# Weight transfers moved away from two rounds of row scatters, and GpSimd's clears and constants moved behind its load requests, in a chunked-attention and top-1 mixture-of-experts kernel

## The chip, the cores and the metric

The kernel runs on one core of a Trainium2 chip. The metric is device time in microseconds of one execution. The time before is 236.27 us, the median of 3 runs (233.84 to 236.61).

The core has five engines with instruction queues of their own: TensorE (PE; its weight loads are shown as PEld), VectorE (DVE), ScalarE (ACT), GpSimd (POOL) and SyncE (SP, which here only issues transfers). Transfers are issued by two of them: SP, whose transfers the profile shows as queue q1, and GpSimd, whose transfers are q0. GpSimd also computes, so a transfer that it issues stands in the same line as its copies and clears.

## The reference

Two parts follow one another.

1. Attention over chunks. For 4 batches and 8 heads, 768 tokens of width 64 are cut into 24 chunks of 32. Each chunk of queries sees 8 memory keys and up to 56 keys around it (16 before the chunk, its own 32, 8 behind), softmax over these, and takes the weighted sum of the values.
2. A mixture of experts over the 3072 resulting tokens of width 512:

```
h_dense = max(x @ w1_dense, 0);  y_dense = h_dense @ w2_dense
logits  = x @ w_gate             # 8 experts
expert  = argmax(logits);  gate = softmax(logits)[expert]
y_moe   = gate * (max(x @ w1[expert], 0) @ w2[expert])
out     = y_dense + y_moe
```

The matrices w1 and w2 of the 8 experts are 512 x 512 each, in float32 in memory; the kernel casts them to bf16 in the transfer.

## The kernel before

**Attention.** The work is cut into 16 pairs of heads (`NPAIR`), four to a batch. The loop `for i in range(last_p)` (L930) computes the values of pair i, the scores of pair i+1 and the transposes of the queries and keys of pair i+2. Ahead of these run the loads: `load_qk(i + 4)` (L1009, issued by GpSimd at L290, two buffers each for q and k) and `load_v(i + 3)` with `load_mem_runs(i + 3)` (L1014, issued by SP). The values of a pair lie in one of four buffers `vw`, 128 partitions wide, with the two heads' keys on 64 partitions each. Three things have to be there before the values' products: the load, the copies that lay overlapping keys a second time (`copy_v`, L410, one head by GpSimd), and zeros in the half of the buffer that belongs to the other head (`clear_side`, L333, a clear of 64 x 1560 elements per head, once per buffer). Before a buffer is loaded again, a one-element clear (L1013, by VectorE) ties the load to the end of the products that read the buffer, so that SP waits for a single engine.

**Routing.** In the second pair of each later batch the kernel routes the batch before it: logits, the chosen expert, the rank of each token within its expert (`rank`, L650). Each token's row (512 values in bf16 with its gate and token number, 1032 bytes) is then scattered to its expert's region of `x_reg` in device memory: `rows_out` (L670), 6 indirect transfers of 128 rows per batch, issued by GpSimd with a tiny clear (`apart`) ahead of each. Batches 0 and 1 (counted from 0) are scattered two transfers per loop turn. The third batch's six (batch 2) all go out in the turn `i == NPAIR - 3` (L1027 to L1038), the last batch's six behind the loop (L1081 to L1086).

**Tiles of 128 tokens.** Slots 0 to 4 are full tiles that batches 0 and 1 can fill, slots 5 to 10 full tiles that batch 2 can fill with them, slots 11 to 26 what is left. `fetch` (L196, issued by SP) loads a tile from `x_reg`. For slots 5 to 10 it is declared independent of the last batch's rows, but it waits for the scatters of batch 2 and for `fill_out` (L687), which writes filler rows. From slot 11 on it waits for the last batch's scatters too. A tile is turned on TensorE (`turn_rows`, L215), goes through the dense layers (`dense_first`, L240; `dense_second`, L256), and behind all 27 dense tiles through the layers of its expert (`expert_first`, `expert_second`, L1159). `rank(B - 1)` (L1079) comes after the logits of the last batch, between the dense layers of slots 2 and 3.

**Weights.** `half_w` (L911) issues the next half of a matrix (256 KB as bf16) on GpSimd. The halves go out in the order w1_dense, w2_dense, w1 of expert 0, 1, and so on. In the kernel before, 16 halves are issued on the way: 2 in turn NPAIR-4, 2 in turn NPAIR-3 ahead of the scatters of batch 2, 4 between these scatters, 2 behind them, 3 at L1069, 2 between the last batch's scatters, 1 at L1097. Where no half stands between two scatters, `pause` (L667) clears 256 elements of one partition. What is left of w1 and all of w2 is loaded in whole matrices (`load_w`, L1184 to L1189, 512 KB each, 10 of them), with at most three outstanding, after a tiny copy by GpSimd (L1181) that waits for slot 12's tile. The experts' products choose a matrix by a register, so the first product of `expert_second` waits for all of w2, and the first copy of `staged` (L1142) for all of w1. Behind the loads GpSimd drains (L1190), and from then on it scatters finished rows to the output (L1169).

**Order.** The program is written out by hand (manual schedule): each engine executes its instructions in the order of the source. Transfers of each issuing engine carry completion semaphores in rotation, eight for GpSimd: its ninth transfer is issued when the first of them has landed.

Of the kernel before, what the change touches and what calls it, by code (L numbers as in the profile page):

```python
# [20 lines left out]
def kernel(  # L21
# [14 lines left out]
    nc = tc.nc  # L36
# [12 lines left out]
    T = S // 128  # L49
# [16 lines left out]
    NPAIR = B * NP  # L66
# [203 lines left out]
    NV = 4  # L270
    vw = [a_const.tile([128, 2, NCH + 1, D + 1], F32, name=f"vw{i}") for i in range(NV)]
# [52 lines left out]
    def clear_side(i, eng, heads=range(2)):  # L324
        for hh in heads:
            p0 = hh * KEYS
            side = vw[i][p0:p0 + KEYS, 1 - hh, :NCH, :]
            if eng is nc.scalar:
                eng.copy(
                    side, zero[p0:p0 + KEYS, None, :].to_broadcast([KEYS, NCH, D + 1])  # L330
                )
            else:
                eng.memset(side, 0.0)  # L333
# [70 lines left out]
    def copy_v(pi, hh, eng):  # L404

        vt = vw[pi % NV]
        p0 = hh * KEYS
        n = CTX - CHUNK
        copy = eng.copy if eng is nc.scalar else eng.tensor_copy
        copy(  # L410
            vt[p0 + CHUNK:p0 + CTX, hh, :NCH, :D], vt[p0:p0 + n, hh, 1:, :D]
        )
# [108 lines left out]
    def scaled(pi):  # L521
        x_p = b_work.tile([128, T, 128], F32, tag="x", name="x", bufs=1)
        rs = b_work.tile([128, 2, TB * 2, 1], F32, tag="rs", name="rs")
        nc.vector.reciprocal(rs, avv[:, :, :, D:D + 1])
        nc.vector.tensor_tensor(  # L525
            x_p.rearrange("p (b t) (h d) -> p b (t h) d", b=2, h=2),
            avv[:, :, :, :D],
            rs.to_broadcast([128, 2, TB * 2, D]),
            ALU.mult,
        )  # L530
        st_[pi]["x"] = x_p
# [48 lines left out]
    def gate_add(pi):  # L580
        b, hp = divmod(pi, NP)
        lgT = bat[b]["lgT"]
        if hp == 0:
            nc.vector.tensor_copy(lgT, g_ps[:96, :])
        else:
            nc.vector.tensor_tensor(lgT, lgT, g_ps[:96, :], ALU.add)
# [291 lines left out]
    def constants_cast():  # L878
        for tf, ti in to_cast:
            nc.gpsimd.tensor_copy(tf, ti)  # L880
        nc.gpsimd.tensor_copy(ohs_of[0][:, T], reg25)
# [29 lines left out]
    def half_w():  # L911
        if not w_halves:
            src, dst = w_todo.pop(0)
            for t in range(0, DT, DT // 2):
                w_halves.append((src[t * 128:(t + DT // 2) * 128], dst[:, t:t + DT // 2]))
        src, dst = w_halves.pop(0)
        nc.gpsimd.dma_start(dst, src.rearrange("(t p) m -> p t m", p=128))

    def row_out():
        if rows_todo:  # L920
            rows_out(*rows_todo.pop(0))
# [3 lines left out]
    def rank_of(b):  # L925
        rank(b)
        rows_todo.extend((b, (t,)) for t in range(T))

    last_p = NPAIR - 1
    for i in range(last_p):  # L930
        b, hp = divmod(i, NP)
        routing = hp == 1 and b > 0
        if routing:
            gate_add(i - 2)
        if i:
            scaled(i - 1)
        if unranked:
            rank_of(unranked.pop())
        if i + 1 < NPAIR:
            if i == 0:  # L940
                clear_side(2, nc.gpsimd, (1,))
            if i == 1:
                slot_no, slot128, desc, pcol, reg25, reg0 = constants()
                constants_cast()
            if i < NPAIR - 2:
                copy_v(i + 1, 0, nc.gpsimd)
            if i == NPAIR - 3:
                for hh in range(2):
                    copy_v(last_p, hh, nc.gpsimd)
            if NPAIR - 4 <= i <= NPAIR - 3:  # L950
                half_w()
                half_w()
            if i == 3:
                spread_mem(1, nc.gpsimd)
            scores_mem(i + 1)
        if i:
            probs_turn(i)
        if i + 1 < NPAIR:
            scores_keys(i + 1)
        if i == 4:  # L960
            tok_ps = token_turn()
        if i == 0:
            clear_side(3, nc.gpsimd, (0,))
        if i == 1:
            clear_side(3, nc.gpsimd, (1,))
        if routing:
            logits(b - 1)
            apart_from_top(b - 1)
        if i:
            copy_v(i, 1, nc.scalar if routing else nc.vector)  # L970
        if i:
            probs_copy(i)
            if i == 4:
                nc.scalar.copy(tok, tok_ps[:, :T])
            gate_part(i - 1)
            record(i - 1)
            if routing:
                chances(b - 1)
        if i + 1 < NPAIR:
            maximum(i + 1)  # L980
            difference(i + 1)
        if i == 0:
            constants_set()
        if routing:
            choose(b - 1)
        elif i > 1:
            gate_add(i - 2)
        values(i, range(TB))
        if i == NPAIR - 6:
            parts = list_whole(ends(B - 2), reg0, lim1, 0, N1)  # L990
        if i == NPAIR - 2:
            done = parts
            parts = list_whole(ends(B - 1), lim1, lim, N1, NA)
            next(parts)
        if i + 2 < NPAIR:
            transpose_qk(i + 2, lambda: exponent(i + 1))
        else:
            exponent(i + 1)
        if i == NPAIR - 6:
            next(parts)  # L1000
            next(parts)
        if i == NPAIR - 5:
            next(parts)
        if i == NPAIR - 4:
            next(parts)
            next(parts)
            bases(0, N1)
        if i + 4 < NPAIR:
            load_qk(i + 4)  # L1009
        for _ in range(2):  # L1010
            row_out()
        if i + 3 < NPAIR:
            nc.vector.memset(vw[(i + 3) % NV][0:1, 0, 1, 0:1], 0.0)  # L1013
            load_v(i + 3)  # L1014
            load_mem_runs(i + 3)
        values(i, range(TB, T))
        if routing:
            ranks(b - 1)
        if i:
            stamp(i - 1)  # L1020
            gate_sum(i - 1)
        if routing:
            if b == B - 1:
                rank_of(b - 1)
            else:
                unranked.append(b - 1)
        if i == NPAIR - 3:  # L1027
            for s in range(N1):
                fetch(s)
            fill_out()  # L1030
            for t in range(T):
                row_out()
                if t < 4:
                    half_w()
                elif t < T - 1:
                    pause()
            for _ in range(2):
                half_w()  # L1038
# [41 lines left out]
    keep_rows(3)  # L1080
    for t in range(T):  # L1081
        rows_out(B - 1, (t,))
        if t < 2:
            half_w()
        elif t < T - 1:
            pause()  # L1086
    dense_second(2)
    for s in range(N1 + 1, N1 + 4):
# [180 lines left out]
```

## Time and profile before

| | |
|---|---|
| median of 3 runs | 236.27 us (233.84 to 236.61) |
| the profiled execution | 236.38 us, of which the trace's span is 234.7 us |
| mean granted TensorE clock | 0.968 |
| PE busy | 199.0 us (85%) |
| DVE busy | 149.0 us (63%) |
| ACT busy | 136.9 us (58%) |
| POOL busy | 145.0 us (62%) |
| transfers | 38.67 MB, mean 165 GB/s; q0 58.0% and q1 28.5% of the DMA engines' span |

How to read it: the span runs from the first to the last instruction of the program; the time of the execution contains 1.7 us more. Busy times are sums over the whole span, and the span has three stages (attention, dense layers, experts) with different limits, so that these shares say little on one stage. The profile's second part cuts the span into 40 equal slices of 5.87 us; there PEclk is the clock that TensorE was granted, in tenths of full speed.

### The profile page before, as it was taken

What the parts mean: (1) busy time and instruction counts of PE and PEld (TensorE: products, weight loads), DVE (VectorE), ACT (ScalarE), POOL (GpSimd) and SP (SyncE); (2) the same over time, 40 slices, a digit from 0 to 9 for tenths busy, and PEclk for the clock granted to TensorE, in tenths of its full rate; (3) what the DMA queues carried; (4) which work ended last, traced back from release to release, by engine and by line L of the source; (5) the groups of instructions that cost most, each with busy time, mean ns of one, the idle gap of its engine ahead of it and who ended that gap; (6) DMA issues with size and microseconds to landing.
All of it is one profiled execution on the core that took longest, in us unless ns stands there. A gap on an engine that the chain in (4) does not pass through costs nothing. (4 is left out here: it accounts for less than half of the span.)

```text
span 234.7 us, 8263 instructions
## 1 busy us (share of the span) xinstructions
PE 199.0 (85%) x3314; PEld 145.9 (62%) x3333; DVE 149.0 (63%) x379; ACT 136.9 (58%) x210; POOL 145.0 (62%) x217
## 2 busy tenths in 40 slices
PE   7678779999988898889840599999999999999990
PEld 2366557667766666668530477777777966666660
DVE  4669848889978899798360341322223758787870
ACT  8678838998997788865620166566666633323320
POOL 7579995445996789588758804123110028988882
PEclk9999979999999999999995599999999999999998
DMA  5999998999999999959999978999990004443333
GB/s 80 178 168 172 167 174 138 171 132 169 182 201 213 156 174 195 221 130 187 215 231 176 282 166 149 200 235 233 217 177 8 3 11 170 180 166 150 142 144 127
DMA packets 53016, 38.67 MB, mean 165 GB/s; under 512 B 30606, under 2 KB 50446, under 8 KB 52976
## 3 DMA queue, kind: packets, MB, share of 16 engines
q0 software_dynamic: 19600, 25.20, 58.0%
q1 hardware_dynamic: 33376, 12.92, 28.5%
q8 instruction: 28, 0.46, 0.9%
q14 instruction: 12, 0.10, 0.2%
HBM read 41.91 MB, written 11.30 MB: 227 GB/s over the span
## 5 line engine op out<-in xcount | busy, mean ns | idle before, releaser
L1169 POOL DMA_INDIRECT out_dram<-y,dst_i x27 | 28.4, 1053 | 18.1 <-DVE y L1163 13.9
L246 ACT ACTIVATE h<-sc 128x512 bf16<-128x512 f32 x27 | 16.2, 598 | 29.5 <-PE sc L240 28.8
L410 POOL COPY vw<-vw 24x1536 f32<-24x1536 f32 x17 | 26.2, 1539 | 8.7 <-DMA vw<-in_v_dram 4.0
L512 PE MATMUL av<-vw,at 128*32 128x130 f32 x768 | 28.9, 277 | 3.0 <-ACT xT L548 1.3
L240 PEld LDWEIGHTS <-w_st 128*128 128x128 bf16 x432 | 25.5, 98 | 4.9 <-DVE w_st L1142 1.9
L674 POOL DMA_INDIRECT x_reg<-rec,row_i x24 | 25.7, 1069 | 4.5 <-issue 4.1
L240 PEld LDWEIGHTS <-w1d 128*128 128x128 bf16 x432 | 26.3, 100 | 1.4 <-issue 0.9
L512 PEld LDWEIGHTS av<-vw,at 128*32 128x32 f32 x768 | 20.1, 108 | 7.4 <-issue 5.4
L246 ACT ACTIVATE xT_B<-sc 128x512 bf16<-128x512 f32 x16 | 9.6, 597 | 25.6 <-PE sc L240 25.6
L1142 DVE COPY w_st<-w_all 128x2048 bf16 x27 | 19.3, 718 | 5.6 <-PE sc L240 4.5
L223 DVE COPY xT_B<-tp 128x512 bf16<-128x512 bf16 x16 | 6.8, 424 | 23.5 <-PE tp L215 19.3
L215 PE MATMUL tp<-identity,xg 128*128 128x128 bf16 x108 | 10.5, 222 | 11.9 <-DMA xg<-x_reg 11.4
L290 POOL DMA_DIRECT2D q_bf<-in_q_dram x16 | 11.4, 712 | 13.5 <-PE tp L424 12.6
L215 PEld LDWEIGHTS <-xg 128*128 128x128 bf16 x108 | 8.1, 99 | 17.4 <-DMA xg<-x_reg 11.6
L256 PE MATMUL av<-w2d,h 128*128 128x512 bf16 x64 | 17.6, 383 | 0.6 <-issue 0.2
L504 ACT COPY at<-at_ps 128x768 f32<-128x768 f32 x16 | 12.8, 800 | 7.7 <-PE at_ps L500 6.5
L240 PE MATMUL sc<-xT_B,w1d 128*128 128x128 bf16 x256 | 16.9, 219 | 0.3 <-DVE xT_B L223 0.3
L240 PE MATMUL sc<-xT_B,w_st 128*128 128x128 bf16 x256 | 16.9, 219 | 0.0
L525 DVE TENSOR_TENSOR x<-av,rs 128x768 f32<-128x768 f32 x16 | 15.3, 958 | 2.0 <-ACT a L494 0.5
L479 DVE TENSOR_REDUCE mx<-sc 128x12 f32<-128x768 f32 x16 | 15.3, 956 | 1.8 <-PE sc L469 1.5
L485 DVE TENSOR_TENSOR dif<-sc,mx 128x768 f32<-128x768 f32 x16 | 15.3, 958 | 1.6
L548 ACT COPY xT<-tp 128x384 f32<-128x384 f32 x32 | 13.9, 485 | 4.1 <-PE tp L545 3.6
(171 smaller groups left out, 445.7 us busy)
## 6 DMA issues: line engine op xcount, KB each, us to landing
vw<-in_v_dram SPq DMA_DIRECT2D x30, 200.0 KB, 5.8
w_all<-in_moe_w_dram POOLq DMA_DIRECT2D x10, 512.0 KB, 10.3
xg<-x_reg SPq DMA_DIRECT2D x27, 129.0 KB, 6.2
q_bf<-in_q_dram POOLq DMA_DIRECT2D x16, 192.0 KB, 6.0
k_bf<-in_k_dram POOLq DMA_DIRECT2D x16, 192.0 KB
w_all<-in_moe_w_dram POOLq DMA_DIRECT2D x12, 256.0 KB, 8.2
vw<-yd_A SPq DMA_DIRECT2D x28, 48.8 KB
x_reg<-fill SPq DMA_DIRECT2D x1, 1032.0 KB
```

The costliest lines, as they stand in the source:

```text
L215: nc.tensor.transpose(xtp[:, d, :], xgb[:, d * 128:(d + 1) * 128], identity)
L240: written(place, nc.tensor.matmul(ph[:, f, :], w[:, d, f * 128:(f + 1) * 128], xT[:, d, :], start=(d == 0), stop=(d == DT - 1),))
L246: was_read(place, nc.scalar.activation(h_sb, ph, AF.Relu))
L256: written(place, nc.tensor.matmul(pd, h_d[:, f, :], w2d_sb[:, f, :], start=(f == 0), stop=(f == FT - 1)))
L410: copy(vt[p0 + CHUNK:p0 + CTX, hh, :NCH, :D], vt[p0:p0 + n, hh, 1:, :D])
L479: nc.vector.reduce_max(mx, scv, axis=AX.X)
L485: nc.vector.tensor_tensor(dif.rearrange("p (b t) (h k) -> p b (t h) k", b=2, h=2), scv, mx.to_broadcast([128, 2, T, KEYS]), ALU.subtract,)
L512: nc.tensor.matmul(av[cc * CHUNK:(cc + 1) * CHUNK, t // TB, (t % TB) * W2:(t % TB + 1) * W2].rearrange("p (h d) -> p h d", h=2), at[:, t, ...
L525: nc.vector.tensor_tensor(x_p.rearrange("p (b t) (h d) -> p b (t h) d", b=2, h=2), avv[:, :, :, :D], rs.to_broadcast([128, 2, TB * 2, D]), ...
L674: inst = nc.gpsimd.indirect_dma_start(x_reg, bass.IndirectOffsetOnAxis(ap=row_i[:, t:t + 1], axis=0), rec[:, t, :], None,)
L1142: nc.vector.tensor_copy(w_st[:, None], w1_all[:, bass.ds(e_dve.pop(s), 1), :, :])
L1169: inst = nc.gpsimd.indirect_dma_start(out, bass.IndirectOffsetOnAxis(ap=dst_i[:, s:s + 1], axis=0), y, None, bounds_check=N_tokens - 1, oo ...
```

## The change

Four edits, all of them of order or place.

- GpSimd's constants (`constants`, `constants_cast`) are computed one loop turn later, in turn 2 in place of turn 1.
- The clears of buffer 3 (`clear_side(3, ...)`, one head each in turns 0 and 1) move from ahead of `load_qk(i + 4)` to behind it, just ahead of `load_v(i + 3)`. In turn 1 the one-element clear that SP's value load waits for is done by GpSimd in place of VectorE, ahead of the moved clear.
- Around batch 2's scatters two halves in place of four go out between the scatters, and the two ahead of them fall away, so that with the two behind them four halves are issued there in place of eight. Pauses stand where halves stood between scatters.
- Between the last batch's scatters there is no half any more, only pauses.

In all 10 halves are issued on the way in place of 16. The six that are missing are three matrices w1, and they are loaded whole: 13 whole loads in place of 10.

```diff
         if i + 1 < NPAIR:
             if i == 0:
                 clear_side(2, nc.gpsimd, (1,))
-            if i == 1:
+            if i == 2:
                 slot_no, slot128, desc, pcol, reg25, reg0 = constants()
                 constants_cast()
...
-            if NPAIR - 4 <= i <= NPAIR - 3:
+            if i == NPAIR - 4:
                 half_w()
                 half_w()
...
-        if i == 0:
-            clear_side(3, nc.gpsimd, (0,))
-        if i == 1:
-            clear_side(3, nc.gpsimd, (1,))
...
         if i + 3 < NPAIR:
-            nc.vector.memset(vw[(i + 3) % NV][0:1, 0, 1, 0:1], 0.0)
+            tie = nc.gpsimd if i == 1 else nc.vector
+            tie.memset(vw[(i + 3) % NV][0:1, 0, 1, 0:1], 0.0)
+            if i < 2:
+                clear_side(3, nc.gpsimd, (i,))
             load_v(i + 3)
             load_mem_runs(i + 3)
...
             for t in range(T):
                 row_out()
-                if t < 4:
+                if t < 2:
                     half_w()
                 elif t < T - 1:
                     pause()
...
     for t in range(T):
         rows_out(B - 1, (t,))
-        if t < 2:
-            half_w()
-        elif t < T - 1:
+        if t < T - 1:
             pause()
```

## Rows read from the trace of the kernel before

**Rows 1.** The page's second part: the granted TensorE clock in 40 slices.
```profile
PEclk9999979999999999999995599999999999999998
```

**Rows 2.** Timeline of PE, us 22 to 43: start us, us, instruction, idle time before it.
```profile
22.22 0.53 PE L424 MATMUL tp<-identity,q_bf 96*64 96x96 bf16 x16
...
27.85 0.53 PE L424 MATMUL tp<-identity,q_bf 96*64 96x96 bf16 x16
...
30.82 0.53 PE L424 MATMUL tp<-halves,k_bf 96*64 96x96 bf16 x16 [2.44 <-DMA k_bf<-in_k_dram]
...
36.93 0.53 PE L424 MATMUL tp<-identity,q_bf 96*64 96x96 bf16 x16
```

**Rows 3.** Timeline of POOL, us 18 to 29.
```profile
18.99 1.40 POOL L333 MEMSET vw<- 64x1560 f32 x1
...
21.33 0.63 POOL L290 DMA_DIRECT2D k_bf<-in_k_dram  x1
21.96 0.30 POOL L865 TENSOR_SCALAR_AFFINE_SELECT upper<-ones 128x128 bf16<-128x128 bf16 x1
...
24.55 1.46 POOL L410 COPY vw<-vw 24x1536 f32<-24x1536 f32 x1
26.07 2.10 POOL L333 MEMSET vw<- 64x1560 f32 x1
28.12 0.66 POOL L290 DMA_DIRECT2D q_bf<-in_q_dram  x1
```

**Rows 4.** Timeline of PE, us 131 to 137, where the dense tiles go on.
```profile
131.48 0.61 PE L215 MATMUL tp<-identity,xg 128*128 128x128 bf16 x4 [11.45 <-DMA xg<-x_reg]
...
134.89 0.39 PE L215 MATMUL tp<-identity,xg 128*128 128x128 bf16 x4
...
136.87 0.39 PE L215 MATMUL tp<-identity,xg 128*128 128x128 bf16 x4
```

**Rows 5.** Waits of SP's queue, us 103 to 142: us in total, times, longest.
```profile
SPq L198 <- DMA x_reg<-rec,row_i: 7.0, 2, 4.2
...
SPq L198 <- DMA x_reg<-fill: 6.0, 1, 6.0
```

**Rows 6.** Timeline of SP, us 112 to 142: the fetches, the first one is slot 5's.
```profile
124.66 17.60 SPq L198 DMA_DIRECT2D xg<-x_reg  x11
```

**Rows 7.** Timeline of POOL, us 103 to 133: halves, pauses, scatters.
```profile
103.34 1.52 POOL L917 DMA_DIRECT2D w2d<-in_moe_w_dense_dram  x2
...
114.53 0.30 POOL L668 MEMSET idle<- 1x256 f32 x1
...
115.03 1.01 POOL L674 DMA_INDIRECT x_reg<-rec,row_i  x1 [0.17 <-issue]
118.60 2.26 POOL L917 DMA_DIRECT2D w_all<-in_moe_w_dram  x3 [2.55 <-DMA x_reg<-rec,row_i]
...
123.86 1.05 POOL L674 DMA_INDIRECT x_reg<-rec,row_i  x1 [0.22 <-issue]
...
132.57 0.97 POOL L674 DMA_INDIRECT x_reg<-rec,row_i  x1 [0.17 <-issue]
```

**Rows 8.** Transfers that write or read the tile x_reg, issue to landing.
```profile
DMA to landing us min/median/max: 3.8/6.2/10.3
```

**Rows 9.** Timeline of DVE: the last batch's row numbers.
```profile
118.22 0.20 DVE L658 TENSOR_REDUCE row_i<-val 128x6 int32<-128x48 f32 x1
```

**Rows 10.** Timeline of POOL, us 141 to 179: the whole matrices' loads.
```profile
141.30 0.18 POOL L1181 COPY scratch<-xg 1x1 f32<-1x1 f32 x1 [6.98 <-DMA xg<-x_reg]
...
151.14 0.75 POOL L118 DMA_DIRECT2D w_all<-in_moe_w_dram  x1 [1.98 <-issue]
...
170.06 0.74 POOL L118 DMA_DIRECT2D w_all<-in_moe_w_dram  x1 [0.28 <-issue]
178.25 0.19 POOL L668 MEMSET idle<- 1x128 f32 x1 [7.46 <-issue]
```

**Rows 11.** Timeline of PE: the first product of an expert's second layer.
```profile
189.43 1.02 PE L1159 MATMUL av<-w_all,xT_A 128*128 x3 [0.34 <-issue]
```

## The prediction, made before the changed kernel was run

> **What bounds the kernel now.** I read the 40 slices first, because the busy shares of the whole span hide the stages. The granted TensorE clock falls to half in two places only, around slice 5 (29 to 35 us) and around slices 21 and 22 (123 to 135 us) [rows 1]. So I looked there in TensorE's timeline. In the first place it waits 2.44 us for the keys of pair 4 [rows 2]. In the second it waits 11.45 us for the tile of slot 5 [rows 4]. These are its two longest waits of the span. I take the time as TensorE's work plus holes, and the change works at both of these.
>
> The second hole, followed back: slot 5's tile is turned at 131.48 [rows 4], its fetch was issued at 124.66 [rows 6], so the transfer took 6.8 us. SP had stood 6.0 us for the filler rows and then 4.2 us for a scatter [rows 5]. This scatter is the sixth of batch 2, issued at 115.03 [rows 7] and landed just before 124.66, that is 9.6 us later. What stands in front of it in GpSimd's queue are six halves and five scatters, all issued from 103.34 on.
>
> The third thing to see is where the halves go if they are taken away. The whole loads start at 141.30, behind slot 12's tile, and GpSimd comes out of its drain at 178.25 [rows 10], which I read as the landing of all of w2. TensorE needs it at 189.43 [rows 11]. There are 11.2 us of slack.
>
> **The first hole (clears and constants).** Pair 4's keys are issued at 21.33, behind the clear of head 0 that begins at 18.99 and takes 1.40 us [rows 3]. Without the clear in front they go out 1.4 us earlier. They were used at 30.82 [rows 2], 9.5 us after the issue. If they keep this time, they land at 29.4, and of the 2.44 us about 1.0 is left: a gain of 1.4. The bounds are 0 (the transfers before them in the engines decide, not the issue) and 2.44. To this comes the clock: from the transposes of pair 4 to those of pair 5 it takes 36.93 - 27.85 = 9.08 us, the turn before took 27.85 - 22.22 = 5.63 [rows 2]; 9.08 - 5.63 - 2.44 = 1.0 us went to the half clock. With a hole of 1 us in place of 2.44 I take 0.8 of it, with bounds 0 and 1.0. Sum: **2.2 us**, from 0 to 3.4.
>
> What moves behind pays nothing that I can see. Pair 5's loads went out at 28.12, behind the constants (21.96 to 24.55, 2.6 us) and the second clear (2.10 us) [rows 3]. They now go out some 3 us earlier, and would be used only at 36.93 less the gain. The value load of turn 1 now waits for GpSimd, which reaches its one-element clear behind pair 5's requests, some 2 us after VectorE did; behind it on SP stand that pair's memory rows and the next value load, needed more than a turn later. The clear of head 1 and then the constants now stand ahead of pair 3's copy. GpSimd does the same work in another order, so the copy ends where it did, within a microsecond or so, while its readers come 2.2 us earlier; the turn in between covers that. If that cover is gone, it takes back at most the gain itself.
>
> **The second hole (four halves fewer).** An issue of a half costs GpSimd 0.76 us, a pause 0.30 [rows 7]. The sixth scatter of batch 2 goes out 1.52 us earlier for the two halves ahead and 0.92 for two pauses in place of halves: 115.03 - 2.4 = 112.6. Its landing is the unknown. By transfer time: the whole loads follow one another in (170.06 - 151.14) / 6 = 3.15 us [rows 10], so a half is 1.6 us and four are 6.3; 124.66 - 6.3 = 118.4. By the issue and the median landing of this tile's transfers, 6.2 us [rows 8], it is 118.8. The bounds are 116.4 and 122.9, with the fastest and slowest, 3.8 and 10.3 [rows 8]. I take 118.5. The filler rows landed at 124.66 - 4.2 = 120.4 [rows 5, 6] behind the same traffic, so they move as well; if they did not, the fetch would go at 120.4.
>
> The fetch took 6.8 us because five halves of the next group stood around it. They still do: the two behind the scatters and the three behind these are issued from 118.60 on before [rows 7], and follow the scatters as closely after. Only the two halves between the last batch's scatters are gone; I take 0.8 us for them, half of one half's transfer. So slot 5 is turned at 118.5 + 6.0 = 124.5 in place of 131.5: **7.0 us**, from 1.8 (fetch at 122.9, 6.8 us) to 11 (fetch at 116.4, 3.8 us [rows 8]). TensorE stops at 120.0 as before. The idle time that is left, 4.5 us, I expect to cost the half clock again, as 2.44 us did. The restart loses (134.89 - 131.48) - (136.87 - 134.89) = 1.4 us to it [rows 4], before and after.
>
> Behind that hole TensorE works without a stop, so the shift lasts if the two later transfers keep up. The last batch's row numbers are ready at 118.4 [rows 9], but its first scatter went at 123.86: GpSimd stood for landings (2.55 us at 118.60 the longest) behind its halves [rows 7]. Now it gets there by about 118.7, and the sixth goes out 0.92 us sooner still, at 126.4 in place of 132.57. Slot 12's tile, and with it the start of the whole loads, comes 6.2 us earlier, at 135.1. Thirteen loads in place of ten: 178.25 - 6.2 + 3 x 3.15 = 181.5 for all of w2. TensorE's need moves to 189.43 - 7.0 = 182.4. So the six halves cost nothing, but the slack falls from 11.2 to 0.9 us. With 37 us / 10 = 3.7 a load, from the whole stretch 141.30 to 178.25, it would be 183.2 and cost 0.8.
>
> The Trainium skill, DMA: Bandwidth & Descriptors, section Issuing engines are not separate DMA queues, says that transfers of all issuing engines run on the same 16 DMA engines and interleave. By it the deferred 1.5 MB are not saved but paid later, which speaks against the change; the load spacing in [rows 10] agrees, and by that spacing the sum stays where it is, since only the slack pays.
>
> **Sum.** 7.0 + 2.2 = 9.2 us off the profiled execution's 236.38 us (span 234.7 and 1.7 around it), which stands 0.1 above the median of the runs: **227.2 us**.
>
> **Rivals.**
> 1. *The first hole stays.* The keys come out of loaded engines 9.5 us after their issue, so something else than the issue may decide. Then only the 7.0 us count: 229.4. For it: the wait is that of a transfer, not of GpSimd.
> 2. *The fetch of slot 5 is held by the filler rows or a slow scatter.* They are issued by SP behind the first fetches, and no edit touches that. With the fetch at 120.4 to 122.9 the second hole gives 4.3 to 1.8 us, say 3.3: 236.4 - 3.3 - 2.2 = 230.9. For it: SP stood longer for them than for the scatter [rows 5]. Against: they share the engines with the halves.
> 3. *The loads of w2 become the bound; this is the case that can end slower.* Its place is the first product of `expert_second`. It decides as soon as all of w2 lands after 182.4. If the loads start only 3 us earlier and take 3.7 each, w2 is there at 186.4, and the gain is 3.0 + 2.2: 231.2. If they did not start earlier and the three ran one after another at 178.25 - 170.06 = 8.2 us each [rows 10], w2 would be there at 202.9, 13.4 us after the need of before: 236.4 + 13.4 - 2.2 = 247.6. Slower than 2% takes w2 at 196.4 or later, 6.0 us for each of the three loads. Against: ten loads follow one another in half of that, beside 15 fetches. The Trainium skill's rule above, on the 16 shared DMA engines, stands behind this rival.
>
> **How the numbers follow.** My forecast has 0.60; it lies between 223.5 and 230.5. Rival 1 has 0.12, rival 2 has 0.14, rival 3 has 0.10 with 0.03 of it slower than before by 2%. Larger gains (no fall of the clock at the restart, another 1.4 us, or a fetch that lands faster) have 0.04, since w2 soon stops them. The range is 223.0 to 232.5: it holds the forecast, rival 1, rival 2 and the nearer part of rival 3. About 2% (4.7 us) can be told from no change: below 231.6 is faster, above 241.0 slower. Faster: 0.60 + 0.12 + 0.04, a little under half of rival 2 and none of rival 3, 0.81. Within: what is left of rivals 2 and 3, 0.15. Slower: 0.04, with something for a mishap that I don't see.
>
> **What would show it.** TensorE's wait for the keys of pair 4 at 1 us or less, and a clock without its first fall. The first fetch behind the filler rows issued near 118.5 less the gain of the first hole, and the turn of slot 5 6 us behind it. The last batch's first scatter right behind its row numbers. Thirteen whole loads 3.15 us apart, and no wait of TensorE at the first `expert_second`; a wait for w_all there is rival 3. The forecast is wrong if GpSimd's order makes pair 3's copy late, or if the scatters land 10 us after their issue with two halves ahead of them too.

## The result, and the profile after

The changed kernel takes 234.23 us (median of 20 runs, 232.01 to 237.66) against 236.60 us for the kernel before (20 runs beside it, 233.84 to 239.61). The ratio is 0.9886, with a 95% interval of 0.9857 to 0.9915: 2.7 us less, where 9.2 were forecast. On three further chips the changed kernel came to 0.9829 (0.9773 to 0.9885), 0.9951 (0.9896 to 1.0006), 0.9881 (0.9802 to 0.996) and again 0.9933 (0.9888 to 0.9979) of the kernel before on the same chip. So it is faster by 0.5 to 1.7%, in one of the five comparisons not clear of no change (0.9951), and by the forecast's 4% in none.

The profiled execution of the changed kernel took 236.18 us (span 234.4), 0.8% above its median; like those of r1, r9 and r17 below it is one of the kernel's slower ones, and that of r14 is not, so that what these show counts where r14 shows it too. Its clock, in 40 slices, against [rows 1]: the first fall comes two slices later, the second is one slice long in place of two.

```profile
PEclk9999999799999999999999599999999999999996
```

The front, in TensorE's timeline (start, duration, instruction, the idle time before it). There is no wait for pair 4's keys [rows 2] in it. A wait stands at pair 6, for the queries and for the keys, and pair 7 (the last line) begins at 50.37 us; in the profile before it was 48.72.

```profile
28.03 0.53 PE L424 MATMUL tp<-identity,q_bf 96*64 96x96 bf16 x16
...
34.43 0.53 PE L424 MATMUL tp<-identity,q_bf 96*64 96x96 bf16 x16
...
41.54 0.53 PE L424 MATMUL tp<-identity,q_bf 96*64 96x96 bf16 x16 [1.70 <-DMA q_bf<-in_q_dram]
43.20 0.85 PE L424 MATMUL tp<-halves,k_bf 96*64 96x96 bf16 x16 [1.12 <-DMA k_bf<-in_k_dram]
50.37 0.53 PE L424 MATMUL tp<-identity,q_bf 96*64 96x96 bf16 x16
```

The scatters, in GpSimd's timeline, against [rows 7, 10]: batch 2's first and sixth scatter, the first of the last batch, the copy that waits for slot 12's tile, the last whole load, and the end of the drain.

```profile
106.30 0.99 POOL L674 DMA_INDIRECT x_reg<-rec,row_i  x1 [0.16 <-POOL scratch L665]
...
114.95 0.98 POOL L674 DMA_INDIRECT x_reg<-rec,row_i  x1 [0.17 <-issue]
...
124.11 1.04 POOL L674 DMA_INDIRECT x_reg<-rec,row_i  x1 [2.79 <-DVE ni L752]
...
138.57 0.18 POOL L1178 COPY scratch<-xg 1x1 f32<-1x1 f32 x1 [5.11 <-DMA xg<-x_reg]
...
176.23 1.20 POOL L118 DMA_DIRECT2D w_all<-in_moe_w_dram  x1 [0.27 <-issue]
184.40 0.48 POOL L668 MEMSET idle<- 1x128 f32 x1 [6.96 <-issue]
```

SP's waits and its timeline, against [rows 5, 6]. SP stands 8.1 us for the filler rows, issued at 109.96, and lets slot 5's fetch go at 125.14; the sixth scatter landed with them, 10.1 us after its issue.

```profile
SPq L198 <- DMA x_reg<-fill: 8.1, 1, 8.1
SPq L198 <- DMA x_reg<-rec,row_i: 5.3, 2, 4.0
```

```profile
109.96 0.41 SPq L688 DMA_DIRECT2D x_reg<-fill  x1
125.14 16.64 SPq L198 DMA_DIRECT2D xg<-x_reg  x11
```

TensorE, against [rows 4, 11]: the hole is 6.72 us long in place of 11.45, but TensorE also came 3.5 us later to it (130.24 - 6.72 = 123.52, against 120.03), and the first product of `expert_second` (last line) is 0.45 us earlier than before. The 3.5 us were lost ahead of the dense tiles: slot 0 is turned at 108.81, against 105.31.

```profile
130.24 0.61 PE L215 MATMUL tp<-identity,xg 128*128 128x128 bf16 x4 [6.72 <-DMA xg<-x_reg]
...
134.05 0.63 PE L215 MATMUL tp<-identity,xg 128*128 128x128 bf16 x4
136.39 0.39 PE L215 MATMUL tp<-identity,xg 128*128 128x128 bf16 x4
...
188.98 1.02 PE L1156 MATMUL av<-w_all,xT_A 128*128 x3 [0.37 <-issue]
```

### The profile page after: what moved, and what is told of

Its sections match the earlier page's. It is cut to its first block, busy times and chain, and to the rows that moved or that the text cites. A ratio compares the mean times of both kernels' runs of the same rounds, so it can differ in the third digit from the quotient of the medians.

```text
span 234.4 us, 8270 instructions
## 1 busy us (share of the span) xinstructions
PE 200.0 (85%) x3314; PEld 146.4 (62%) x3333; DVE 148.4 (63%) x378; ACT 137.2 (59%) x210; POOL 144.0 (61%) x222
## 5 line engine op out<-in xcount | busy, mean ns | idle before, releaser
L512 PE MATMUL av<-vw,at 128*32 128x130 f32 x768 | 29.7, 281 | 3.9 <-ACT xT L548 1.4
L410 POOL COPY vw<-vw 24x1536 f32<-24x1536 f32 x17 | 24.8, 1461 | 10.4 <-DMA vw<-in_v_dram 7.1
L223 DVE COPY xT_B<-tp 128x512 bf16<-128x512 bf16 x16 | 6.8, 424 | 23.5 <-PE tp L215 19.4
L290 POOL DMA_DIRECT2D q_bf<-in_q_dram x16 | 11.5, 717 | 14.0 <-PE tp L424 12.9
L256 PE MATMUL av<-w2d,h 128*128 128x512 bf16 x64 | 18.1, 391 | 0.6 <-issue 0.2
L432 ACT COPY qT<-tp 128x768 bf16<-128x768 bf16 x16 | 12.7, 797 | 6.9 <-PE tp L424 6.5
```

The costliest lines, as they stand in the source:

```text
L256: written(place, nc.tensor.matmul(pd, h_d[:, f, :], w2d_sb[:, f, :], start=(f == 0), stop=(f == FT - 1)))
L410: copy(vt[p0 + CHUNK:p0 + CTX, hh, :NCH, :D], vt[p0:p0 + n, hh, 1:, :D])
L512: nc.tensor.matmul(av[cc * CHUNK:(cc + 1) * CHUNK, t // TB, (t % TB) * W2:(t % TB + 1) * W2].rearrange("p (h d) -> p h d", h=2), at[:, t, ...
```

## The experiments

Kernels of one group ran on one chip, beside runs of the kernel before; the groups ran on four chips, so that times of different groups are only compared through their ratios.

**First group: the two parts of the change, and the filler rows** (kernel before there: 243.09 us). The changed kernel itself:

> The changed kernel once more, for a second profile and for a time on the same chip as its parts. Theory A (the fetch of slot 5 waits for the filler rows, and the first hole comes back at pair 6): 0.98 to 0.995 of before, TensorE's wait for slot 5's tile 6 to 8 us, a wait for pair 6's queries or keys of 2 us or more. Theory B (the halves in front of the scatters and the clears in front of the loads decide, as predicted): below 0.975, no wait for pair 6.

Only the edits of clears and constants (the halves as before):

> Only the edits at GpSimd's clears and constants; all 16 halves stay where they were. Theory A: 0.99 to 1.005, the wait for pair 4's keys gone and one of about the same size at pair 6, whose requests now go out behind the constants. Theory B: 2.2 us less (0.99), no new wait.

Only the edits of the halves (clears and constants as before):

> Only the edits at the halves; clears and constants as before. Theory A: 1.5 to 4 us less (0.983 to 0.994), SP stands longer for the filler rows than for the last scatter of batch 2, and slot 5's fetch goes out no earlier than 120 us. Theory B: 7 us less (0.97), the fetch goes out at 118.5.

These edits, and the filler rows issued in turn 6:

```diff
+        if i == 6:
+            fill_out()
...
-            fill_out()
             for t in range(T):
                 row_out()
```

> As the kernel with only the edits at the halves, and in addition the filler rows are written in loop turn 6 in place of turn 13, ahead of the first fetches. Theory A: 3 us or more less than without the move (0.96 to 0.975 of before), since the fetch of slot 5 waits for the scatters alone and these no longer share the engines with 1 MB of filler rows. Theory B: no different from the kernel with the halves' edits alone, or up to 2 us slower, since the filler rows now stand in the way of the loads of the attention.

Measured: 0.9829 (0.9773 to 0.9885), 0.9971 (0.9921 to 1.002), 0.9885 (0.9837 to 0.9933) and 1.0018 (0.9981 to 1.0055). What the change brings comes from the halves; of the clears and constants alone no gain can be told from none. Theory B's 0.97 for the halves is missed, and so is theory A's 0.96 to 0.975 without the filler rows. Yet the filler rows do what A says to the scatter: in the third run the sixth scatter landed 5.2 us after its issue (117.17 to 122.32), in the fourth 3.5 us (118.80 to 122.34). The time does not follow, because TensorE has no hole at slot 5 in either: it comes there only at 129.05 and 130.19. The first run's profile has no hole there either (129.08) and waits 1.44 us at pair 6, so that its time is theory A's and its waits are neither's.

In front, the second run has no wait for pair 4's keys. TensorE's transposes, pairs 3, 4, 5, 6 and 7, and its one longer wait in that stretch, for memory rows of pair 1's values; the third run, with the old order, waits there too (1.56 us):

```profile
23.36 0.88 PE L512 MATMUL av<-vw,at 128*32 128x130 f32 x24 [2.30 <-DMA vw<-in_mem_v_dram]
24.17 0.53 PE L424 MATMUL tp<-identity,q_bf 96*64 96x96 bf16 x16
30.70 0.53 PE L424 MATMUL tp<-identity,q_bf 96*64 96x96 bf16 x16
35.79 0.53 PE L424 MATMUL tp<-identity,q_bf 96*64 96x96 bf16 x16
41.13 0.53 PE L424 MATMUL tp<-identity,q_bf 96*64 96x96 bf16 x16
48.20 0.53 PE L424 MATMUL tp<-identity,q_bf 96*64 96x96 bf16 x16
```

**Second group: both kernels profiled side by side, and no halves near batch 2's scatters** (before: 237.42 us). In the last two, all four halves of the dense matrices go out in turn NPAIR-4, no half among batch 2's scatters, none behind them or at L1069, and six behind the last batch's scatters; the last one also issues the filler rows at the end of turn NPAIR-4.

```diff
             if i == NPAIR - 4:
-                half_w()
-                half_w()
+                for _ in range(4):
+                    half_w()
...
-                if t < 2:
-                    half_w()
-                elif t < T - 1:
+                if t < T - 1:
                     pause()
-            for _ in range(2):
-                half_w()
...
-    for _ in range(3):
-        half_w()
...
-    half_w()
+    for _ in range(6):
+        half_w()
```

> The kernel before itself, for a profile on the chip of the three runs beside it. Theory A (the scatters of batch 2 and the fetch behind them share the DMA engines with the halves and the filler rows; each that is taken away lets them land sooner): TensorE waits 6 to 11 us for slot 5's tile, and the sixth scatter of batch 2 lands 6 to 10 us after its issue. Theory B (the hole is only moved: TensorE itself comes later to slot 5 when the traffic around it changes): the same hole here; what differs is seen in the other three.

> The changed kernel, for a profile beside the kernel before. Theory A: the fetch of slot 5 goes when the filler rows land, 15 us after their issue, within 1.5 us of the time at which it goes before. Theory B: TensorE stops for slot 5 at least 3 us later than before, and its hole is smaller by as much. Both: the wait for the keys of pair 4 is gone and one of 1 us or more stands at a pair between 5 and 7.

> No half is issued among batch 2's scatters or behind them until the last batch's scatters are out; the two of w2_dense go ahead of them, the six of w1 behind. The filler rows stay where they are. Theory A: the sixth scatter lands about 2 us sooner after its issue, the fetch of slot 5 lands 3 us after its issue in place of 5 to 6.8, TensorE restarts 4 to 6 us earlier than in the changed kernel: 0.965 to 0.98 of before. Theory B: TensorE's arrival at slot 5 is the limit and no traffic is left to blame: 0.98 to 0.99, as the changed kernel.

> As the run before it, and the filler rows are written four pairs' turns from the end, behind the last value load, in place of behind the first fetches. Theory A: the sixth scatter lands 3 to 4 us after its issue, the fetch of slot 5 goes at once behind it, no hole is left at slot 5 beyond 1 us: 0.955 to 0.97 of before. Theory B: as the run before it, 0.98 to 0.99, since TensorE comes late by itself.

Measured: 238.74 us and 230.97 us in the one run of each; 0.987 (0.9773 to 0.9968) for the third; a median of 241.18 us (4 runs, 237.90 to 243.35) for the fourth, which has no interval and so gives no verdict. The second is the run in which the forecast's chain can be seen as it was written. SP, then TensorE, in the profile of the changed kernel:

```profile
106.30 0.41 SPq L688 DMA_DIRECT2D x_reg<-fill  x1
118.97 3.21 SPq L198 DMA_DIRECT2D xg<-x_reg  x6
```

```profile
124.63 0.40 PE L215 MATMUL tp<-identity,xg 128*128 128x128 bf16 x4 [2.49 <-DMA xg<-x_reg]
...
183.35 1.02 PE L1156 MATMUL av<-w_all,xT_A 128*128 x3 [2.53 <-issue]
```

The fetch goes at 118.97 (forecast 118.5), slot 5 is turned at 124.63 (forecast 124.5), and the clock holds behind it (slot 6 is turned 1.99 us later). Theory A's fetch, within 1.5 us of that of before (126.74), and theory B's stop, 3 us later than before (122.14 against 123.12), are both wrong here, and there is no wait at pairs 5 to 7. But TensorE then waits 2.53 us at the first `expert_second`. GpSimd came out of its drain at 182.80, 0.55 us ahead: this is the wait for w2, rival 3. Without the halves, in the third run, there is no hole at all, and the wait for w2 grows; SP's fetches, then TensorE:

```profile
110.77 0.41 SPq L688 DMA_DIRECT2D x_reg<-fill  x1
119.25 4.42 SPq L198 DMA_DIRECT2D xg<-x_reg  x6
```

```profile
186.60 1.02 PE L1151 MATMUL av<-w_all,xT_A 128*128 x3 [3.00 <-issue]
```

There the sixth scatter landed 3.3 us after its issue and slot 5's tile 2.1 us after its fetch (121.40), against 6.6 and 5.6 us in the run with the halves. So theory A is right on the transfers; its 0.965 to 0.98 misses the measured 0.987, whose interval begins at 0.9773. In the fourth run the filler rows stand ahead of the fetch of slot 0 (TensorE waits 4.28 us there) and the wait for w2 is 6.00 us.

**Third group: w2, a place for the halves, and the front** (before: 242.33 us). The changed kernel again; w2 of three experts cleared in place of loaded; the halves of the second group's third kernel, but five between the last batch's scatters and three behind; and the values of one head left out in pairs 4 to 7.

```diff
-    for e in range(E):
+    for e in range(E - 3):
         w_todo.append((moe_w2[e], w2_all[:, e]))
...
+    for e in range(E - 3, E):
+        nc.gpsimd.memset(w2_all[:, e], 0.0)
     nc.gpsimd.drain()
```

```diff
         rows_out(B - 1, (t,))
         if t < T - 1:
-            pause()
+            half_w()
...
-    for _ in range(6):
+    for _ in range(3):
         half_w()
```

```diff
-        for hh in range(2):
+        for hh in range(1 if 4 <= pi <= 7 else 2):
             h = 2 * hp + hh
```

> The changed kernel again, beside the three below. Theory C (the change does take most of the hole at slot 5 away, and the first product of the experts' second layers then waits for the landing of w2): TensorE restarts at slot 5 within 3 us of its stop or soon after, its wait at the first expert_second is 1 to 3 us, and that product starts 1.2 us behind the last whole load's landing; 0.975 to 0.99 of before. Theory A (the hole stays, held by the filler rows and slow scatters): the hole at slot 5 is 5 us or more and there is no wait for w2; 0.985 to 0.995.

> The changed kernel with the w2 of the last three experts not loaded but cleared by GpSimd (it leaves these three loads out): ten whole loads as before the change. Theory C: no wait at the first expert_second, 1 to 2.5 us less than the changed kernel beside it, 0.965 to 0.98. Theory A: w2 was never the limit, the same as the changed kernel within 0.5%.

> As the run in which no half goes among or behind batch 2's scatters (two of w2_dense ahead), but of the halves behind, five now go between the last batch's scatters and three after them, so that 12 whole loads are left. Theory C: no hole at slot 5, the whole loads start within 1 us of the changed kernel's and end 2 to 3 us sooner, the wait for w2 is 0 to 1.5 us, and the time is 0.965 to 0.98, below the changed kernel. Theory A: the halves beside the fetches of slots 5 to 10 make these late again, and it is no better than the changed kernel, 0.985 to 0.995.

> The changed kernel with the values of the second head of pairs 4 to 7 not loaded (200 KB of each pair's 400 left out, the buffer keeps older values). Theory D (in the first 45 us the transfers themselves are the limit, and the hole only moves when GpSimd's order changes): TensorE's waits for keys, queries and values behind pair 3 vanish, pair 7's transposes start 2 to 4 us before those of the changed kernel beside it. Theory E (the order of GpSimd's requests is the limit): the waits between pairs 4 and 7 stay within 0.7 us. The time falls by less than the front gains, 0.97 to 0.985, if w2 holds the end.

Measured: 0.9951 (0.9896 to 1.0006), 0.9888 (0.9818 to 0.9958), 1.0223 (1.0108 to 1.0338), and 266.42 us for the last. In the first two neither profile shows a wait for w2, nor a hole at slot 5: TensorE comes to it at 132.11 and 126.59. That is neither theory C nor theory A. The 0.6% between them lies inside the intervals and settles nothing. The third was expected to be the best and is the slowest of the three: with halves between them the last batch's scatters are 2.1 us apart in place of 1.5, slot 11's fetch goes at 143.77, and TensorE stands 3.91 us for it. In the fourth the values left out lead to other experts, and the experts' stage takes 26 us longer (187.31 to 256.73, against 193.99 to 237.72), so that only its front is read: behind 23.31 us (a wait of 1.63) no wait of 0.9 us or more is left in front of pair 7, which begins at 47.03, against 53.55 in the changed kernel beside it. This fits theory D, but four of the other kernels with the new order begin pair 7 by 47.5 as well, so that this run alone does not prove it.

**Fourth and fifth group: does TensorE itself come late, and does one whole load less help** (before: 241.02 and 243.01 us, one chip). The last kernel is the changed one with three halves in place of one at L1094:

```diff
     next(parts)
-    half_w()
+    for _ in range(3):
+        half_w()
```

> The kernel before, for a profile on the chip of the three runs beside it. Theory F (halves in flight beside the last pair's products and the first dense tiles slow TensorE itself, without a wait that the profile can name; before, the same happens inside the hole at slot 5 and costs nothing): from the turn of slot 1 to TensorE's stop for slot 5 it takes 11.9 us, or, where the changed kernel stalls, also 14 us or more. Theory G (the chip): 14 us or more on a slow chip for every kernel, 11.9 on a fast one.

> The changed kernel beside the others. Theory F: where TensorE has no hole of 2 us or more at slot 5, it takes 14.5 us from the turn of slot 1 to slot 5 in place of 11.9 and 11 us from there to slot 8 in place of 6 to 7.5. Theory G: the same as the kernel before on this chip. Theory C (w2): where it does not stall, it waits 1 to 3 us at the first expert_second. 0.98 to 0.995 of before.

> No half among or behind batch 2's scatters until the last batch's scatters are out (measured once before at 0.987). Theory F: 11.9 us from slot 1 to slot 5, 6 to 6.6 us from slot 5 to slot 8, on any chip, and a wait of 2 to 4 us for w2 at the end; 0.98 to 0.99. Theory G: on a slow chip it stalls as the changed kernel does, 14 us and 11 us.

> The changed kernel with three halves in place of one behind the last batch's scatters, so that twelve whole loads are left in place of thirteen. Theory C: w2 lands 2 to 3 us sooner, its wait falls below 1 us, 0.5 to 1% less time than the changed kernel beside it where that one waits for w2. Theory F: where the changed kernel stalls at slots 5 to 8 instead, w2 is no limit and the time is the same within 0.5%, or worse by what slot 11's fetch loses beside the two halves (up to 2 us).

> The changed kernel, for more timed runs and one more profile. Theory C (the fetch of slot 5 gains 3 to 6 us, then w2 holds the end): hole at slot 5 below 4 us, a wait of 1 to 3 us at the first expert_second, 0.975 to 0.985 of before. Theory H (TensorE stalls for want of instructions as soon as no hole covers it): no hole, 14.5 us or more from the turn of slot 1 to slot 5, 11 us from slot 5 to slot 8, no wait for w2, 0.985 to 0.995. Theory A (filler rows and scatters hold the fetch): the hole stays at 5 us or more, 0.985 to 0.995.

> Three halves in place of one behind the last batch's scatters, twelve whole loads (measured once at 0.987). Theory C: w2 lands 2 to 3 us sooner than in the changed kernel beside it, and the time is 0.5 to 1% below it. Theory H or A: the same as the changed kernel within 0.5%.

Measured: 239.72 us for the kernel before (one run); changed 0.9881 (0.9802 to 0.996) and 0.9933 (0.9888 to 0.9979); without the halves 1.0195 (1.0094 to 1.0297); three halves behind 0.9869 (0.9802 to 0.9936) and 0.9927 (0.9878 to 0.9976). One whole load less is as fast as the changed kernel within what can be told; it still waits 2.02 us for w2 in r16, where theory C had less than 1, and not at all in r18. Taking the halves away, 0.987 in the second group, loses 2% here.

The two profiles of one chip that settle most are these: TensorE from slot 1 to slot 8 in the kernel before, and in the changed one.

```profile
110.10 0.38 PE L215 MATMUL tp<-identity,xg 128*128 128x128 bf16 x4
110.41 1.56 PE L512 MATMUL av<-vw,at 128*32 128x130 f32 x48
...
115.60 0.38 PE L215 MATMUL tp<-identity,xg 128*128 128x128 bf16 x4 [0.29 <-ACT xT L548]
...
128.79 0.61 PE L215 MATMUL tp<-identity,xg 128*128 128x128 bf16 x4 [5.81 <-DMA xg<-x_reg]
...
137.03 0.39 PE L215 MATMUL tp<-identity,xg 128*128 128x128 bf16 x4
```

```profile
110.74 0.39 PE L215 MATMUL tp<-identity,xg 128*128 128x128 bf16 x4
111.06 1.30 PE L512 MATMUL av<-vw,at 128*32 128x130 f32 x37
112.61 0.31 PE L512 MATMUL av<-vw,at 128*32 128x130 f32 x2 [0.25 <-issue]
113.35 0.42 PE L512 MATMUL av<-vw,at 128*32 128x130 f32 x4 [0.44 <-issue]
114.08 0.43 PE L512 MATMUL av<-vw,at 128*32 128x130 f32 x4 [0.30 <-issue]
114.81 0.27 PE L512 MATMUL av<-vw,at 128*32 128x130 f32 x1 [0.30 <-issue]
...
119.09 0.38 PE L215 MATMUL tp<-identity,xg 128*128 128x128 bf16 x4 [0.29 <-ACT xT L548]
...
126.33 0.38 PE L215 MATMUL tp<-identity,xg 128*128 128x128 bf16 x4
126.55 1.06 PE L240 MATMUL sc<-xT_A,w1d 128*128 128x128 bf16 x16
...
129.25 0.38 PE L215 MATMUL tp<-identity,xg 128*128 128x128 bf16 x4 [0.48 <-DVE ol L760]
...
133.21 1.89 PE L256 MATMUL at_ps<-w2d,h 128*128 128x512 bf16 x4 [2.26 <-issue]
134.89 0.63 PE L215 MATMUL tp<-identity,xg 128*128 128x128 bf16 x4
...
137.57 0.39 PE L215 MATMUL tp<-identity,xg 128*128 128x128 bf16 x4
```

The stretch takes 26.93 us with a hole of 5.81 us and 26.83 us with none. In the changed kernel the last pair's 48 products, 1.56 us of work before, start as before, and the last 11 run in groups of one to four with idle time between them that has no releaser; then VectorE's list of tiles (L749 to L765), which before was made inside the hole, stands ahead of slot 5's copy; then 2.26 us without a releaser, and the half clock behind it (0.63 us for a turn in place of 0.39). The two executions took 239.72 and 239.93 us, so this pair shows how the gain is lost, and not where the chip's 0.7 to 1.2% come from.

On the 2.26 us a row of ScalarE, in the changed kernel, says more:

```profile
132.56 0.60 ACT L246 ACTIVATE h<-sc 128x512 bf16<-128x512 f32 x1 [4.88 <-PE sc L240]
```

This activation writes slot 4's `h`, which the product at 133.21 reads, and it ends at 133.16: TensorE waited for it. (In r15 and r16 the profile itself names it, with 2.19 and 1.49 us.) ScalarE had stood 4.88 us for TensorE's scores, although TensorE's row for slot 4's scores ends at 126.55 + 1.06 = 127.61. The same wait, 2.22 to 2.27 us, ends within 0.1 us of this activation in r1, r3, r4, r9, r10, r17 and r18. Whether the scores came late or the row ends too early (the profile's ends of products are modelled), no row says.

Theory G's form of this (on such a chip every kernel takes 14 us or more from slot 1 to the stop) is wrong: before it was 12.9. Theory F's cause is not enough: the kernel without halves (r15) takes 11.92 us from slot 1 to slot 5 and waits 3.58 us for w2, as F said, but stalls elsewhere. It took 8.26 us from slot 0 to slot 1 (2.83 before), with a wait of 3.11 us without a releaser, which ends with VectorE's `x` (L525, to 114.89), and 9.69 us from slot 5 to slot 8, where F had 6 to 6.6.

Theory H's signs are all there in r17: no hole, 14.52 us from slot 1 to slot 5, 11.44 us from there to slot 8, no wait for w2, 0.9933. Its cause, a want of instructions, is not shown by that: the profile's page lists the same 28 and 12 transfers of instructions (q8 and q14, 0.56 MB) before and after, and no run changes them. It stays an untested rival.

## Why the prediction was wrong

Stage times of ten profiles, in us from the start of the span; TensorE stops at slot 5's turn less the idle time before it, a hole of 0 is a turn without a wait, and the last column is the first product of `expert_second`, with its wait where it has one of over 0.5 us. Profiles of one chip stand together.

| profile | slot 0 turned | fetch of slot 5 | TensorE stops | hole | slot 1 to slot 8 turned | first expert_second |
|---|---|---|---|---|---|---|
| before | 105.31 | 124.66 | 120.03 | 11.45 | 30.70 | 189.43 |
| after | 108.81 | 125.14 | 123.52 | 6.72 | 26.73 | 188.98 |
| before (r5) | 108.41 | 126.74 | 123.12 | 9.61 | 29.95 | 191.76 |
| after (r6) | 106.78 | 118.97 | 122.14 | 2.49 | 20.97 | 183.35, 2.53 |
| before (r13) | 107.27 | 122.91 | 122.98 | 5.81 | 26.93 | 187.63 |
| after (r14) | 107.80 | 119.09 | 126.33 | 0 | 26.83 | 188.18 |
| after (r17) | 111.21 | 122.00 | 128.57 | 0 | 25.96 | 190.64 |
| front alone (r2) | 107.72 | 123.70 | 123.67 | 6.43 | 27.39 | 188.56 |
| after (r1) | 110.42 | 121.78 | 129.08 | 0 | 27.09 | 191.11 |
| after (r9) | 114.73 | 124.88 | 132.11 | 0 | 25.75 | 193.99 |

**The first hole.** The forecast took it from one profile, and of the five with the old order only that one waits for pair 4's keys. r5, r13 and r3 wait at pair 5 in its place, r4 at neither; here r5, then r13:

```profile
38.26 0.53 PE L424 MATMUL tp<-halves,k_bf 96*64 96x96 bf16 x16 [1.13 <-DMA k_bf<-in_k_dram]
```

```profile
34.76 0.53 PE L424 MATMUL tp<-identity,q_bf 96*64 96x96 bf16 x16 [1.04 <-DMA q_bf<-in_q_dram]
```

So that no kernel with the new order waits for them is not shown to be the edit's work. The step that failed is the next one, "What moves behind pays nothing that I can see". The constants now stand ahead of pair 6's requests, which in the profile shown first go at 32.55 and 33.55 and are used 9.0 and 9.7 us later, and six of the fifteen kernels with the new order wait 1.1 to 2.1 us there (after, r1, r7, r9, r11, r17), none of the five with the old one. Pair 7 begins at 48.72, 51.23, 47.08, 50.55 and 49.75 in the five profiles with the old order (49.5 in the mean) and at 45.5 to 53.6 in fourteen with the new one (48.6; r12, which leaves values out, is not counted): 0.9 us less, and well within the spread. By 0.9971 (0.9921 to 1.002) of 243.09 us for these edits alone, the 2.2 us are 0.7, between a gain of 1.9 and a loss of 0.5. Rival 1 had that price, though the hole did not stay: it moves from execution to execution.

**The second hole, the transfers.** This part held in five of the changed kernel's six profiles. The sixth scatter went out at 112.35 in r6 (forecast 112.6); from issue to landing it took 4.0 to 6.6 us in those five (5.9 forecast), and 10.1 only in the one shown first, where the filler rows landed with it: rival 2, and one of the prediction's own signs of being wrong. Measured from the turn of slot 0, the fetch went 15.6 to 19.4 us later with the old halves (before, r5, r13, r2) and 10.2 to 12.2 us later in those five, where the forecast has 118.5 - 105.31 = 13.2. That fetch and turn in r6 came within 0.5 us of the forecast is partly luck: the prediction lets them go earlier still by the gain in front, and r6 came to slot 0 1.47 us later than before. Also the last batch's first scatter went as forecast, right behind its row numbers (121.33 and 120.53 in r6).

**The second hole, TensorE.** Here is the error that cost most: "TensorE stops at 120.0 as before" and "Behind that hole TensorE works without a stop". I priced the hole at its length. In the changed kernel's six profiles TensorE comes to slot 5 between 122.1 and 132.1, and in four of them it has no hole left and nothing gained: slot 1 to slot 8 takes 25.8 to 27.1 us, as it does with a hole in r13 and r2, on two of the same chips. Without its hole r13 takes 26.93 - 5.81 = 21.12 us, so that in r14, on the same chip, 5.7 us of stalls took the place of a hole of 5.81. In r6 the same work, without hole and stalls, takes 20.97 - 2.49 - 0.63 (a wait for w2_dense) = 17.85 us, 8 to 9 less than in those four. Part of the stalls is named (the list on VectorE, the wait for ScalarE's `h`, the half clock); why ScalarE came late, and what the last pair's products wait for, is not shown: it is not the halves alone, since r15 has none, and not the chip alone, since r13 and r2, with the old halves, have no gap at these products. (r11, without halves, takes 6.5 us from slot 5 to slot 8, but 6.4 from slot 0 to slot 1.) The other part of the late arrival lies ahead of slot 0: in the profile shown first it is the whole 3.5 us, in r14 0.53, while the forecast had TensorE 2.2 us earlier. Pair 7 accounts for 1.65 us of the 3.5; the cause of the rest is open.

**w2.** I put the landing of w2 at 181.5 and TensorE's need at 182.4. In r6 the drain ends at 182.80 and the need would have been at 183.35 - 2.53 = 180.82. The loads took (182.10 - 137.78) / 13 = 3.41 us each, between my two values, and their start came at 137.3, not 135.1, since slot 12's tile landed 4.5 us after its fetch. Rival 3 was thus true, at 2.5 us, in the one run in which the rest of the forecast stood, and a slack of 0.9 us out of terms of 3 us each was none. The same wait is 2.02 in r16, 3.00 in r7, 3.58 in r15 and 6.00 in r8, and in r7 again the product starts 0.64 us behind the drain (185.96).

**Together.** On one chip and in one execution each (r6 beside r5) the chain of the forecast does stand, less w2: 230.97 and 238.74 us. As a rule it does not: the first hole moves, TensorE comes late to the second and stalls in its place, and 2.7 us are left of 9.2. No pair of profiles shows these 2.7 us: before and after took 236.38 and 236.18 us, r13 and r14 239.72 and 239.93. The Trainium skill, DMA: Bandwidth & Descriptors, section Issuing engines are not separate DMA queues, which the forecast set against its sum, is borne out: the same fetch took 2.1 us with no halves in flight, 5.6 with five of them and 6.8 in [rows 4, 6], though SP issues it and GpSimd the halves.

No version beat the changed kernel by more than can be told; three halves behind the last scatters, at 0.9869 and 0.9927, came nearest.

## What to carry to other kernels

The length of a wait on the critical engine is an upper bound of what its removal brings, not its price: ask which other work now ends inside the wait (here a list on VectorE and stalls that no row explains) and price the stretch by the same work in a place without a wait. When loads are moved behind a stage, sum them up to the point of use, with the slower of the measured spacings; a slack smaller than one term of that sum is not a cover. And profile the kernel before and the changed one more than once on the same chip before a single trace decides.

## What the runs showed of the hardware that was not expected

- TensorE can idle without any releaser in the trace: at the last pair's products 0.24 to 0.44 us between groups of two to six products, 0.71 to 0.77 us apart. These ten profiles of kernels with the two halves of w2_dense between the scatters, on three chips, all have four or five such gaps (r1, r3, r4, r9, r10, r12, r14, r16, r17, r18); in two more the same code has none (after, r6). What it waits for is open.
- ScalarE and VectorE can begin 4 to 5 us behind the row that writes their input: in r14 ScalarE's activation at 132.56, behind scores whose row ends at 127.61; in r15 VectorE's L524 at 113.59, behind products whose row ends at 109.13. TensorE then waits for them, 2.26 and 3.11 us, and the profile names no releaser.
- The kernel before has medians of 236.6, 237.4, 241.0, 242.3, 243.0 and 243.1 us on the chips and occasions of these runs, a spread wider than the effect of the change.
- Six scatters and 1032 KB of filler rows land in 3.3 us from the last issue with no halves in flight (r7), and in 10.1 us beside two halves among the scatters and five behind (after); with the same halves the other five profiles of the changed kernel have 4.0 to 6.6 us.
